# Batch 1 of a decay attention with its softmax weights turned by TensorE and float32 values

## The chip, the core and the metric

The kernel runs on one core of a Trainium2 chip. The core has five engines with a queue each, which run in order and wait for one another by semaphores: TensorE (PE, matmuls into PSUM), VectorE (DVE), ScalarE (ACT), GpSimd (POOL) and SyncE (SP, which here issues nearly all DMAs). The metric is the device time of one execution in microseconds; smaller is better.

## The reference

Attention with a decay for 8 batches of 8 heads, 576 tokens, 64 columns each, and then a feed-forward layer (FFN) over all 4608 tokens:

```python
scores = scale * np.matmul(q, k.transpose(0, 1, 3, 2))
log_f = np.log(np.clip(f, 0.0001, 1.0))
cum = np.cumsum(log_f, axis=-1)
decay = cum[:, :, :, None] - cum[:, :, None, :]
causal = np.triu(np.ones((S, S), dtype=bool), k=1)
scores = np.where(causal, -1000000000.0, scores + decay)
scores = scores - np.max(scores, axis=-1, keepdims=True)
attn = np.exp(scores)
attn = attn / (np.sum(attn, axis=-1, keepdims=True) + 1e-09)
...
x = np.ascontiguousarray(attn_out.transpose(0, 2, 1, 3)).reshape(B * S, H * D)
h = x @ w_in
g = np.maximum(h, 0.0) + np.log1p(np.exp(-np.abs(h)))
return (g @ w_out).astype(np.float32)
```

Here `w_in` is 512x2048 and `w_out` 2048x512. Everything is float32.

## The kernel before

**Attention.** Work is cut into jobs. Batch 0 has jobs of its own (`first`, `second`, `rest`, called plain): its scores are unsplit float32 products (L951), its softmax weights stay unnormalised, TensorE turns them with an identity matrix (`turn`, L1110), a copy brings them from PSUM to SBUF (`keep`, L1120, recorded as L254), and `output_tiled` multiplies them with float32 values (L1164) on two halves of the PE columns, 64 columns each. The division by the sums comes last (L1188).

From batch 1 on a job is one head (`whole`). q and k are split into a high and a low part by casts (L254) and subtractions (L907, L913), and the scores of a tile of query rows are two matmuls (L956, L957). `row_min` on DVE (L961) finds the row's extreme, ACT makes the exponentials and their sums (L989), `over` the reciprocals (L1002 to L1005). Then `turn_tile` normalises and splits each weight into two fp16 planes: the first part on ACT, POOL or DVE (L1037, L1039), the second on DVE (L1042). One DMA transpose per head (L1053, on SP's queue) turns both planes. The values are split in fp16 parts too (`split_v`, L874, L876, L880), with a scale by the largest value of each head, which `peak` finds with a DMA load and DVE reductions one batch ahead (L704 to L742). `output` multiplies (L1224, eleven matmuls), ACT scales one half of the result (L1244), DVE adds the other (L1248).

**FFN.** Tokens are taken in blocks: two of 128 in float32 (L1348, L1460), one of 256, then eight of 512. From the 256 block on each product is three matmuls of split operands: up (L1367, with the low weights from DRAM, `wl`), the activation on ACT and DVE (L1400 to L1420), down (L1441). A block can start when the attention of all its tokens is done. So block 256 to 511 needs batch 0, and the first block of 512 needs all heads of batch 1.

**Order.** Every operation is recorded in a plan with its predecessors, a cost and the buffers that it takes; `Plan.run` (L118) goes through the next 700 of them, always emits the one that can start earliest, and gives it to the engine that ends it first where there is a choice. What is emitted is a fixed order for each engine.

## Time and profile before

| | us |
|---|---|
| median of three runs | 1163.02 |
| lowest, highest | 1162.47, 1169.52 |
| the profiled execution | 1157.93 |
| its span, first to last instruction | 1156.1 |
| PE busy | 1094.2 |
| DVE busy | 882.3 |
| ACT busy | 808.6 |
| POOL busy | 231.6 |

The profile is one execution. Busy times count a matmul from its start to a modelled end, and neighbours overlap, so PE can be shown busy without running at its best. The clock column is what the throttle granted to TensorE, 1.00 being full speed. The rows that the prediction uses stand below, with the line numbers of the kernel before.

### The profile page before, as it was taken

To read this page: it belongs to the slowest core of one execution; us is meant where nothing else is said; L and a number is where in the kernel's file an instruction comes from. 1 tells how busy PE (TensorE), PEld (TensorE's weight loads), DVE (VectorE), ACT (ScalarE), POOL (GpSimd) and SP (SyncE) were. 2 spreads that over 40 slices of the span, in tenths; PEclk is the share of its full clock that TensorE was granted. 3 is DMA by queue.
4 is the path that set the end of the run, shared out by engine and by line. 5 is a ranking of instruction groups with operands and counts; after the bars stand their busy time and mean duration, and the time that the engine had idled before them with its cause. 6 is when DMAs were issued, how large, how long until landed. Compare 5 with 4: busy or idle time off the path is not lost. (4 is left out here: it accounts for less than half of the span.)

```text
span 1156.1 us, 17362 instructions
## 1 busy us (share of the span) xinstructions
PE 1094.2 (95%) x5452; PEld 849.8 (74%) x5452; DVE 882.3 (76%) x2169; ACT 808.6 (70%) x1867; POOL 231.6 (20%) x274
## 2 busy tenths in 40 slices
PE   8999787679998899999999999999999999999998
PEld 6776575557777677777777777777777777888886
DVE  7889899798888999989989888988898763223222
ACT  6888675657776677877778868877677775445444
POOL 3133222112221321212232121232233110000000
PEclk9999988888999899999999999999999999999999
DMA  9867688888977887869777977697669652112110
GB/s 246 247 201 225 199 207 212 203 204 188 213 177 168 183 214 185 200 156 227 182 168 172 228 177 176 151 221 172 154 143 219 152 121 90 43 55 73 55 55 37
DMA packets 278092, 193.55 MB, mean 167 GB/s; under 512 B 225216, under 2 KB 247008, under 8 KB 278000
## 3 DMA queue, kind: packets, MB, share of 16 engines
q1 hardware_dynamic: 277832, 192.29, 67.7%
q8 instruction: 43, 0.70, 0.2%
q14 instruction: 49, 0.40, 0.1%
q10 hardware_dynamic: 168, 0.15, 0.0%
HBM read 114.16 MB, written 14.83 MB: 112 GB/s over the span
## 5 line engine op out<-in xcount | busy, mean ns | idle before, releaser
L989 ACT ACTIVATE p<-s,negm 128x288 f32<-128x288 f32 (+7 forms) x384 | 184.2, 482 | 111.4 <-DVE negm L961 107.7
L1367 PE MATMUL h<-xh,wih 128*128 128x512 f32 (+1 forms) x576 | 228.0, 399 | 12.8 <-ACT p L989 4.8
L1367 PE MATMUL h<-xl,wih 128*128 128x512 f32 (+1 forms) x576 | 221.7, 388 | 2.3 <-DVE xl L1319 2.3
L1441 PE MATMUL acc<-woh_dt_float32r,gl 128*128 128x512 f32 x544 | 215.8, 397 | 7.4 <-DVE gl L1420 7.4
L1039 POOL TENSOR_SCALAR cross<-p,rsum 128x64 f16<-128x64 f32 (+4 forms) x146 | 139.8, 975 | 414.3 <-DVE rsum L1005 161.0
L1441 PE MATMUL acc<-woh_dt_float32r,gh 128*128 128x512 f32 x544 | 218.6, 402 | 2.3 <-ACT gh L254 1.4
L1441 PE MATMUL acc<-wol_dt_float32r,gh 128*128 128x512 f32 x544 | 215.0, 395 | 0.0
L1412 DVE SCALAR_TENSOR_TENSOR e<-h,e 128x512 f32<-128x512 f32 x136 | 93.2, 685 | 129.4 <-ACT e L1406 128.8
L1042 DVE SCALAR_TENSOR_TENSOR cross<-p,rsum,cross 64x64 f16<-64x64 f32 (+1 forms) x336 | 179.3, 569 | 14.4 <-POOL cross L1039 8.5
L961 DVE CUSTOM_DVE_ANT_0 s<-s,cmask 128x288 f32<-128x288 f32 (+6 forms) x320 | 135.6, 439 | 28.8 <-PE s L957 16.4
L1400 ACT ACTIVATE e<-h 128x512 f32<-128x512 f32 x144 | 85.6, 595 | 99.4 <-PE h L1367 96.3
L1367 PE MATMUL h<-xh,wl 128*128 128x512 f32 (+1 forms) x576 | 150.7, 384 | 1.1 <-DMA wl<-wil_d 1.1
L1367 PEld LDWEIGHTS h<-xh,wih 128*128 128x128 f32 x576 | 111.4, 193 | 34.8 <-ACT p L989 6.0
L1441 PEld LDWEIGHTS acc<-woh_dt_float32r,gl 128*128 128x128 f32 x544 | 103.7, 191 | 34.5 <-DVE gl L1420 12.1
L1367 PEld LDWEIGHTS h<-xl,wih 128*128 128x128 f32 x576 | 111.4, 193 | 22.2 <-DVE xl L1319 4.4
L254 ACT CAST gh<-e 128x512 fp32r<-128x512 f32 x128 | 79.2, 619 | 66.7 <-DVE e L1412 66.1
L1367 PEld LDWEIGHTS h<-xh,wl 128*128 128x128 f32 x576 | 106.5, 191 | 23.9 <-DMA wl<-wil_d 1.3
L1441 PEld LDWEIGHTS acc<-woh_dt_float32r,gh 128*128 128x128 f32 x544 | 103.9, 191 | 22.1 <-ACT gh L254 3.0
L956 PE MATMUL s<-T 128*64 128x64 f32 x336 | 105.8, 326 | 13.8 <-ACT e L1403 3.9
L1420 DVE TENSOR_TENSOR gl<-e,gh 128x512 fp32r<-128x512 f32 x136 | 93.8, 689 | 31.0 <-ACT gh L254 30.3
L1441 PEld LDWEIGHTS acc<-wol_dt_float32r,gh 128*128 128x128 f32 x544 | 103.9, 191 | 18.1
L957 PE MATMUL s<-T 68*64 68x64 f32 x336 | 100.5, 304 | 5.9 <-DVE T L913 5.6
(127 smaller groups left out, 1664.2 us busy)
## 6 DMA issues: line engine op xcount, KB each, us to landing
wl<-wil_d SPq DMA_DIRECT2D x72, 512.0 KB
raw<-in_qkT SPq DMA_DIRECT2D x112, 288.0 KB
vr<-in_vR SPq DMA_DIRECT2D x64, 160.0 KB
vp<-in_vR SPq DMA_DIRECT2D x28, 320.0 KB
out<-ob SPq DMA_DIRECT2D x35, 256.0 KB
T<-T SPq DMA_DIRECT2D x56, 144.0 KB
sto<-in_w_out SPq DMA_DIRECT2D x11, 512.0 KB
sti<-in_w_in SPq DMA_DIRECT2D x9, 512.0 KB
```

Source lines behind the costliest of these rows:

```text
L254: (e.tensor_copy if hasattr(e, "tensor_copy") else e.copy)(out, in_)
L956: e.matmul(o, qA[:, q0:end], kA[:, a:z], start=True, stop=False)
L957: e.matmul(o, qB[0:ST, q0:end], kB[0:ST, a:z], start=False, stop=True)
L961: e.tensor_tensor_reduce(out=box["o"], in0=box["o"], in1=cmask[0:n_q, right - w : right], scale=-0.125, scalar=m0 if i else 3.0e38, op0=AL ...
L989: e.activation(o, box["o"], AF.Exp, bias=m1, scale=-1.0, accum_out=acc)
L1039: e.tensor_scalar(to1, of, f_, None, ALU.mult)
L1042: e.scalar_tensor_tensor(to2, of, f_, to1, ALU.mult, ALU.subtract)
L1367: e.matmul(o, l, r, start=m == 0, stop=m == 11)
L1400: e.activation(box["e"], st["h", u], AF.Abs)
L1412: e.scalar_tensor_tensor(o, st["h", u], 0.0, box["e"], ALU.max, ALU.add)
L1420: e.tensor_sub(box["l"], box["e"], box["h"].bitcast(F32))
L1441: e.matmul(st["acc", tt], l, r[fc], start=first and m == 0, stop=last and m == 2,)
```

## The change

The eight heads of batch 1 become jobs `mixed`. Their scores, exponentials and sums stay as they were. Then the weights are normalised in place in float32 (`scale`: five instructions per head, on DVE, ACT or POOL), turned by TensorE in four banks per head (fifteen transposes), and copied to SBUF (four copies). The values are loaded into a float32 buffer and not split; `output_tiled` multiplies them in nine float32 matmuls on two column tiles, queries 0 to 383 on one and 384 to 575 on the other, and two copies (`take`) bring the result to its place. The fp16 planes, the DMA transpose, the split of the values and the search for their peaks are gone for batch 1, and stay for batches 2 to 7. The first bank has a tile of 68 rows of its own (`p64`), for the first 64 keys.

```diff
+    def mixed(h):
+        banks = [[(0, 0, 64, 0, 0), (512, 512, S, 0, 4)], [(0, 64, S, 0, 0)], [(128, 128, S, 0, 1)],
+                 [(256, 256, S, 0, 2), (384, 384, S, 0, 3)]]
+        return whole(1, h) | dict(
+            banks=banks, groups=[(0, 384, 0, 0), (384, S, 1, 0)],
+            puts=[(0, 384, h, 0), (64, S - 384, h, 384)],
+        )
...
+        mixed_ = not plain and b == 1
...
+                if mixed_:
+                    vtag = "vhl"
+                elif plain:
...
-            split_v()
+            if not mixed_:
+                split_v()
...
+            st["norm"] = []
+            for ti, (_, n_q, _, pi, po) in enumerate(tiles):
+                def scale(e, ti=ti, n_q=n_q, pi=pi, po=po):
+                    a, f_ = pt[pi][0:n_q, po : po + ends[ti]], rs[0:n_q, ti : ti + 1]
+                    if hasattr(e, "activation"):
+                        e.activation(a, a, AF.Copy, scale=f_)
+                    else:
+                        e.tensor_scalar(a, a, f_, None, ALU.mult)
+                st["norm"].append([add(scales(ends[ti]), scale, after=[r])])
...
+                        if small:
+                            x, one = pt[pi][:, c : c + ST], halves
+                            if key == 0:
+                                x, one = x[0:ST], ident[0:ST, 0:ST]
+                            blocks.append((x, key // 8, one))
...
-                    steps[bi].append(mm)
+                    steps[bi if plain else 0].append(mm)
...
-                            st["vr"][m["vc"][0]]["v"][:, m["vc"][1], :],
-                            m["p"]["p"][:, m["o"] : m["o"] + m["z"] - m["a"]],
+                            st["vr"][m["vc"][0]]["v"][0 : m["rows"], m["vc"][1], :],
+                            m["p"]["p"][0 : m["rows"], m["o"] : m["o"] + m["z"] - m["a"]],
...
+                def take(e, r=r, w=w, h=h, tok=tok):
...
+                    copy(e, to, box["ps"][r : r + 64, 0:w])
+                on = [on_act(w, psum=True), on_dve(w)]
+                d = add(on, take, after=before + x_taken.get(b, []), takes=takes)
...
-    jobs += [whole(b, h) for b in range(1, B) for h in range(H)]
+    jobs += [mixed(h) for h in range(H)]
+    jobs += [whole(b, h) for b in range(2, B) for h in range(H)]
...
-            if nstart <= n + H + 1 < len(jobs):
+            if nstart + H <= n + H + 1 < len(jobs):
```

How the order moves, at three places. The line numbers of the changed kernel are larger: its L965 to L971 are scores, L1145 turns, L1201 float32 values, L1421 and L1495 the FFN's up and down, L1036 is `scale`, L1003 the exponentials.

PE, third head of batch 1, before: the FFN's products (`acc`) and the scores (`s`) of the next head stand ahead of the fp16 values (`o_0`, `o_1`), which read the planes in `cross`.

```order
L1441 MATMUL acc_1_1788<-woh_dt_float32r,gl_2_1984 128x512
L956 MATMUL s_4_288_2057<-T_1297 128x288
L957 MATMUL s_4_288_2057<-T_1297 128x288
L1224 LDWEIGHTS v_17_1691
L1224 MATMUL o_0_2064<-cross,v_17_1691 128x64
```

The same engine in the changed kernel, between the heads of batch 1: the last values of one head (`o`), then the turning of the next (`b_0`, `b_1`), then a score of the one after.

```order
L1201 MATMUL o_1887<-cross,vr_1463 64x192
L1201 MATMUL o_1887<-cross,vr_1463 64x64
L1145 MATMUL b_0_1904<-ident,p_68_96 68x68
L1145 MATMUL b_0_1904<-halves,p_640_100 68x128
L1145 MATMUL b_1_1908<-ident,p_256_97 128x128
L1145 MATMUL b_1_1908<-ident,p_384_98 128x128
L1145 MATMUL b_1_1908<-ident,p_512_99 128x128
L1145 MATMUL b_1_1908<-ident,p_640_100 128x128
L970 MATMUL s_3_0_1917<-T_1080 128x448
```

The turning has come into PE's queue, ahead of scores that used to follow the values directly.

ACT at about the same head, before: first parts of the planes (`cross`) among exponentials, the result's scaling (`x`) and a cast of k or q.

```order
L989 ACTIVATE p_512_99,lsum_82<-s_3_0_2034,negm_78 128x448
L1037 ACTIVATE cross<-p_256_92,rsum_89 128x2x128
L1037 ACTIVATE cross<-p_384_93,rsum_89 128x3x128
L1244 ACTIVATE x_1_1646<-o_0_2064,v_down_113 64x64
L1037 ACTIVATE cross<-p_512_94,rsum_89 128x4x128
L254 CAST T_1078<-raw_2028 128x576
```

ACT in the changed kernel: normalising in place (`p`), and copies of turned banks (`cross<-b`).

```order
L1003 ACTIVATE p_640_100,lsum_80<-s_4_288_1788,negm_76 128x288
L254 CAST T_1307<-raw_1775 128x576
L1036 ACTIVATE p_68_96<-p_68_96,rsum_88 64x64
L254 COPY cross<-b_3_1840 128x512
L1036 ACTIVATE p_384_98<-p_384_98,rsum_88 128x320
L1036 ACTIVATE p_512_99<-p_512_99,rsum_88 128x448
L1036 ACTIVATE p_640_100<-p_640_100,rsum_88 128x576
L1003 ACTIVATE p_68_91,lsum_81<-s_0_0_1860,negm_77 64x64
```

Four of this head's five normalisations stand on ACT, where three first parts stood.

PE where the first block of 512 tokens begins (`h_0`), before: behind the values of batch 1's last head (`o_1`) and three scores of a head of batch 2.

```order
L1224 MATMUL o_1_2621<-cross,v_21_2218 128x64
L956 MATMUL s_0_0_2648<-T_1078 64x64
L957 MATMUL s_0_0_2648<-T_1078 64x64
L956 MATMUL s_1_0_2651<-T_1078 128x192
L957 MATMUL s_1_0_2651<-T_1078 128x192
L956 MATMUL s_2_0_2654<-T_1078 128x320
L957 MATMUL s_2_0_2654<-T_1078 128x320
L1367 MATMUL h_0_2663<-xh_2527,wih 128x512
```

The same place in the changed kernel: four scores of the same head of batch 2, and the last products of the block of 256 (`acc`).

```order
L970 MATMUL s_3_0_2688<-T_1080 128x448
L971 MATMUL s_3_0_2688<-T_1080 128x448
L1495 MATMUL acc_0_1874<-woh_dt_float32r,gh_7_2678 128x512
L1495 MATMUL acc_0_1874<-wol_dt_float32r,gh_7_2678 128x512
L1495 MATMUL acc_0_1874<-woh_dt_float32r,gl_7_2681 128x512
L1495 MATMUL acc_1_1875<-woh_dt_float32r,gh_7_2678 128x512
L1495 MATMUL acc_1_1875<-wol_dt_float32r,gh_7_2678 128x512
L1495 MATMUL acc_1_1875<-woh_dt_float32r,gl_7_2681 128x512
L1421 MATMUL h_0_2706<-xh_2629,wih 128x512
```

What has moved is the end of the block of 256, which is now the last thing ahead of the block of 512; the head of batch 2 has come about as far.

## Rows read from the trace of the kernel before

**Rows 1.** The page of the profile, busy tenths of PE and the granted TensorE clock in 40 slices of the span (one slice is 28.9 us).

```profile
PE   8999787679998899999999999999999999999998
...
PEclk9999988888999899999999999999999999999999
```

**Rows 2.** Busy time by stage (the view by windows): bounds in us, length, busy time of PE, PE's weight load, DVE, ACT and POOL with the number of instructions, the mean granted TensorE clock, the DMA engines' share, GB/s.

```profile
50.00:100.00 50.00, 49.29 (x318) 36.03 (x317) 45.24 (x103) 41.72 (x91) 14.71 (x18) 0.97 0.73 228
125.00:256.00 131.00, 101.86 (x534) 77.47 (x534) 116.36 (x312) 85.67 (x223) 30.69 (x33) 0.84 0.84 204
256.00:300.00 44.00, 38.73 (x179) 29.57 (x180) 37.67 (x88) 32.30 (x75) 10.12 (x10) 0.92 0.83 189
300.00:450.00 150.00, 142.51 (x686) 110.54 (x685) 132.51 (x329) 109.67 (x263) 37.66 (x42) 0.98 0.82 191
450.00:900.00 450.00, 440.98 (x2173) 344.51 (x2171) 394.09 (x995) 346.67 (x829) 110.88 (x112) 1.00 0.78 183
```

**Rows 3.** The same view for the stage 125 to 256 us, cut near the starts of its DMA transposes.

```profile
125.00:140.00 15.00, 13.11 (x60) 8.09 (x61) 13.98 (x44) 9.41 (x29) 4.96 (x6) 0.89 0.66 189
140.00:157.00 17.00, 11.35 (x53) 8.78 (x52) 16.42 (x43) 10.04 (x25) 2.38 (x3) 0.70 0.75 186
157.00:171.00 14.00, 13.63 (x92) 11.64 (x91) 12.24 (x33) 13.45 (x34) 5.18 (x5) 1.00 0.96 227
171.00:185.00 14.00, 7.97 (x40) 5.37 (x39) 13.57 (x36) 9.45 (x26) 4.79 (x3) 0.76 0.89 218
185.00:199.00 14.00, 10.87 (x62) 8.45 (x61) 12.94 (x33) 7.97 (x19) 3.17 (x4) 1.00 0.87 212
199.00:213.00 14.00, 9.18 (x52) 6.75 (x51) 10.39 (x31) 9.69 (x26) 3.64 (x4) 0.76 0.83 201
213.00:227.00 14.00, 12.29 (x81) 10.86 (x79) 9.35 (x30) 7.13 (x22) 1.98 (x2) 0.88 0.93 200
227.00:241.00 14.00, 10.67 (x47) 7.93 (x48) 13.13 (x32) 9.73 (x23) 2.85 (x3) 0.76 0.83 188
241.00:256.00 15.00, 12.79 (x63) 9.61 (x61) 14.34 (x39) 8.81 (x27) 1.74 (x3) 0.89 0.91 219
```

**Rows 4.** SyncE's queue in order of time: the DMA transposes of the first and of the last head of batch 1 (start us, us).

```profile
143.03 4.62 SPq L1053 DMA_TRANSPOSE cross<-cross  x1
...
241.36 5.31 SPq L1053 DMA_TRANSPOSE cross<-cross  x1
```

**Rows 5.** What PE waited for between 125 and 256 us (the view of waits: us in total, times, longest).

```profile
PE s L957 <- DVE T L913: 5.2, 5, 3.3
PE o L1224 <- DMA cross<-cross: 4.7, 2, 2.7
PE s L956 <- ACT e L1403: 3.9, 1, 3.9
```

**Rows 6.** DVE between 125 and 256 us, grouped by line: instructions, then busy us and mean ns of one, then idle time before them and what ended it.

```profile
L1042 DVE SCALAR_TENSOR_TENSOR cross<-p,rsum,cross 128x512 f16<-128x512 f32 (+4 forms) x54 | 27.0, 539 | 2.8 <-POOL cross L1039 1.8 <-ACT cross L1037 0.8
...
L1248 DVE SCALAR_TENSOR_TENSOR x<-o,v_down,x 64x64 f32<-64x64 f32 (+1 forms) x15 | 7.5, 498 | 0.9 <-ACT x L1244 0.6
...
L880 DVE SCALAR_TENSOR_TENSOR v<-vr,v_up,v 128x320 f16<-128x320 f32 x10 | 5.4, 542 | 0.0
```

**Rows 7.** ACT between 125 and 256 us, grouped by line and shape; same columns.

```profile
L1037 ACT ACTIVATE cross<-p,rsum 128x512 f16<-128x512 f32 x11 | 7.8, 717 | 0.1
...
L1244 ACT ACTIVATE x<-o,v_down 64x512 f32<-64x512 f32 x7 | 4.8, 684 | 1.4 <-PE o L1224 1.2
...
L1244 ACT ACTIVATE x<-o,v_down 64x64 f32<-64x64 f32 x8 | 2.5, 310 | 1.6 <-PE o L1224 1.5
...
L1037 ACT ACTIVATE cross<-p,rsum 64x64 f16<-64x64 f32 x3 | 1.0, 340 | 0.0
```

**Rows 8.** Copies of turned weights out of PSUM (batch 0) and casts of q and k, whole span, grouped by line and shape; same columns.

```profile
L254 ACT CAST T<-raw 128x576 fp32r<-128x576 f32 x60 | 39.2, 667 | 7.2 <-PE s L956 3.6 <-DMA raw<-in_qkT 2.7 <-DMA vr<-in_vR 0.8
...
L254 ACT COPY cross<-b 128x512 f32<-128x512 f32 x9 | 5.2, 578 | 2.8 <-PE b L1113 2.8
L254 DVE COPY cross<-b 128x512 f32<-128x512 f32 x7 | 4.7, 675 | 0.0
```

**Rows 9.** PE in order of time where a head of batch 0 is turned, and where its values are multiplied (start us, us, what, number).

```profile
105.24 0.28 PE L1110 MATMUL b<-ident,p 128*128 128x128 f32 x1
...
105.46 0.93 PE L1110 MATMUL b<-ident,p 128*128 128x128 f32 x7
106.23 1.02 PE L1460 MATMUL acc<-wol_dt_float,g 128*128 128x512 f32 x2
...
112.60 1.31 PE L1164 MATMUL o<-cross,vr 128*64 128x192 f32 x18
```

**Rows 10.** The granted clock while PE ran those (the view by windows).

```profile
105.00:109.00 4.00, 3.49 (x23) 2.56 (x22) 3.97 (x12) 4.00 (x11) 2.05 (x4) 1.00 0.93 291
```

**Rows 11.** PE in order of time at the values of the first head of batch 1.

```profile
153.97 0.33 PE L1224 MATMUL o<-cross,v 128*128 128x64 f16 x2
...
156.00 1.45 PE L1224 MATMUL o<-cross,v 128*128 128x512 f16 x9
```

**Rows 12.** PE in order of time where the first block of 512 tokens begins.

```profile
260.13 0.50 PE L1367 MATMUL h<-xh,wih 128*128 128x512 f32 x1 [2.67 <-ACT xh L254]
261.78 0.80 PE L1367 MATMUL h<-xl,wih 128*128 128x512 f32 x1 [1.15 <-DVE xl L1319]
```

More of the change, by code (lines that the diff above doesn't have):

```diff
@@ L298, in tile_decay_attention_softplus_ffn @@
                 x32=2, wl=2, vhl=3, vraw=1, vpk=1, raw=1)
-    plan = Plan(BUFS | dict(bank=6, acc=2, acc2=0, T0=4, stat=4, p=2, xh0=1, xh1=1, xl0=1, ph=3, pl=3, one=2, pp=1, pT=1))
+    plan = Plan(BUFS | dict(bank=6, acc=2, acc2=0, T0=4, stat=4, p=2, xh0=1, xh1=1, xl0=1, ph=3, pl=3, one=2, p64=2, pp=1, pT=1))
     add, give = plan.add, plan.give
@@ L350, in tile_decay_attention_softplus_ffn @@
     rsum = [cpool.tile([P, 5], F32, name=f"rsum{i}") for i in range(4)]
-    PW = [64] + [128 * (i + 1) for i in range(1, 5)]
+    PW = [ST] + [128 * (i + 1) for i in range(1, 5)]
     ps = [[cpool.tile([P, w], F32, name=f"p{i}_{w}") for w in PW] for i in range(2)]
@@ L387, in tile_decay_attention_softplus_ffn @@
         one=[cross[:, 3200 + P * i : 3200 + P * i + P] for i in range(2)],
+        p64=[cross[:, i : i + P] for i in (3456, 3712)],
     )
@@ L1002, in over @@
                 e.scalar_tensor_tensor(a, a, 1e-9, z, ALU.add, ALU.add)
-                if not plain:
+                if not plain and not mixed_:
                     e.tensor_scalar(a, a, 1.0 / UP, None, ALU.mult)
@@ L1013, in finish_stats @@
             st["over"] = r
+            if not mixed_:
+                return
+            st["norm"] = []
[7 more added lines that the diff above has]
+                st["norm"].append([add(scales(ends[ti]), scale, after=[r])])
+            give("stat", [x for xs in st["norm"] for x in xs])
         def turn_tile(ti):
@@ L1069, in weights @@
                 w += hi - lo
+            small = mixed_ and bi == 0
             blocks, need = [], []
             for ti, (q0, n_q, k0, pi, po) in enumerate(tiles):
-                for key, lo, hi, _, at in reversed(spans):
+                for key, lo, hi, _, at in spans if small else reversed(spans):
                     if q0 < hi and q0 + n_q > lo and k0 <= key:
@@ L1081, in weights @@
                         c = po + key - k0
-                        one = halves if second else ident
-                        blocks.append((pt[pi][:, c : c + P], at, one))
+                        if small:
[3 more added lines that the diff above has]
+                            blocks.append((x, key // 8, one))
+                        else:
+                            one = halves if second else ident
+                            blocks.append((pt[pi][:, c : c + P], at, one))
                         need += st["norm"][ti]
             box = {}
-            sums = job["sums"].get(bi, [])
+            sums = job["sums"].get(bi, []) if plain else []
             if sums:
@@ L1113, in turn @@
                     e.transpose(box["ps"][:, at1 + at : at1 + at + m], one, ident[0:m, 0:m])
-            tag = tags[bi] = ("ph", "pl")[count["p"] % 2]
-            count["p"] += 1
+            tag = tags[bi] = "p64" if small else ("ph", "pl")[count["p"] % 2]
+            count["p"] += not small
+            rows = ST if small else P
             def keep(e):
                 box["p"] = slice_of(tag, used[bi])[:, 0:w]
-                copy(e, box["p"], box["ps"][:, 0:w])
+                copy(e, box["p"][0:rows], box["ps"][0:rows, 0:w])
             need = list(dict.fromkeys(need)) + halves_set
@@ L1129, in weights @@
                 give("p", st["turned"])
-                give("stat", st["turned"])
+                if plain:
+                    give("stat", st["turned"])
             on = [on_act(w, psum=True), on_dve(w)]
@@ L1134, in weights @@
             for key, lo, hi, vc, at in spans:
-                parts.append((lo, hi, bi, vc, at, box, ready))
+                parts.append((lo, hi, bi, vc, at, box, ready, rows))
         def output_tiled():
@@ L1142, in output_tiled @@
                 todo.sort(key=lambda x: (max(x[0], g0) > g0, x[2]))
-                for lo, hi, bi, vc, at, pbox, ready in todo:
+                for lo, hi, bi, vc, at, pbox, ready, rows in todo:
                     a, z = max(lo, g0), min(hi, g1)
@@ L1180, in output_tiled @@
             puts = []
-            for r, rows, c, w, bi, o, h, tok in job["puts"]:
+            for r, w, h, tok in [] if plain else job["puts"]:
+                def take(e, r=r, w=w, h=h, tok=tok):
+                    if b not in x_of:
+                        x_of[b] = buf("x32", [P, NCC, S], f"x32_{b}")
+                    to = x_of[b][64 * (h % 2) : 64 * (h % 2) + 64, h // 2, tok : tok + w]
+                    copy(e, to, box["ps"][r : r + 64, 0:w])
+                takes = () if b in x_taken else ("x32",)
+                on = [on_act(w, psum=True), on_dve(w)]
+                d = add(on, take, after=before + x_taken.get(b, []), takes=takes)
+                x_taken.setdefault(b, [d])
+                puts.append(d)
+                wrote.setdefault(b, []).append((tok, tok + w, d))
+            for r, rows, c, w, bi, o, h, tok in job["puts"] if plain else []:
                 def put(e, r=r, rows=rows, c=c, w=w, bi=bi, o=o, h=h, tok=tok):
@@ L1198, in output_tiled @@
             give("att", puts, back(box, "ps"))
-            if quad:
+            if mixed_:
+                give("T", st["scores"])
+                give("vhl", before)
+            elif quad:
                 s_of[heads[0]] = s_of[heads[2]] = st["scores"], before
@@ L1276, in attention @@
             s=[lambda ti=ti: stat_tile(ti) for ti in range(nt)],
-            w=[lambda bi=bi: weights(bi) for bi in range(len(banks))] if plain
+            w=[lambda bi=bi: weights(bi) for bi in range(len(banks))] if plain or mixed_
             else [lambda ti=ti: turn_tile(ti) for ti in range(nt)],
-            o=[output_tiled] if plain else [lambda gi=gi: output(gi) for gi in range(len(groups))],
+            o=[output_tiled] if plain or mixed_ else [lambda gi=gi: output(gi) for gi in range(len(groups))],
         )
```

3 lines of the change are left out of this document (1 added, 2 removed).

## The prediction

> **What bounds the kernel now.** I read the page's slices first, then busy times by stage, then what PE waits for. The slices show PE at nine or ten tenths from about 290 us to the end, and at six to nine tenths with a reduced clock between about 125 and 290 us [rows 1]. By stage this is plainer. From 300 to 900 us PE is busy 142.51 of 150 us and 440.98 of 450 us at a clock of 0.98 and 1.00, so there the kernel is as long as PE's work. From 125 to 256 us PE is busy 101.86 of 131 us at a mean clock of 0.84, while DVE is busy 116.36, which is 89% [rows 2]. That stage is the attention of batch 1: its eight DMA transposes are issued between 143.03 and 241.36 us [rows 4], one head in 14 us ((241.36 - 143.03) / 7). The only FFN work that may run beside it is the block of 256 tokens and what is left of the two float32 blocks. The first block of 512 waits for batch 1 and starts at 260.13 us [rows 12].
>
> What PE waits for in the stage is mostly DVE and the transposes: 5.2 us for the low part of k (L913), 4.7 us for `cross` from the DMA, 3.9 us once for a stretch that an exponential of the FFN ended [rows 5]. Each pause has a second price. In the pieces with pauses (140 to 157, 171 to 185, 199 to 213, 227 to 241) the granted clock was 0.70 to 0.76, a mixture of its two levels, 1.2 and 2.4 GHz; in the dense piece from 157 to 171 it was 1.00 [rows 3]. Busy time times clock, summed over the nine pieces, gives 87.5 us of PE work at full clock in 131 us, a share of 67%. So some 43 us of PE are lost in this stage, and DVE sets its pace.
>
> **The change, part by part.** Counting the two programs' orders, the changes are of batch 1 alone.
>
> DVE loses 48 second parts of planes at 0.539 us, 16 additions of results at 0.498 and 8 low parts of values at 0.542 [rows 6]: 25.9 + 8.0 + 4.3 = 38.2 us. It gains 22 copies from PSUM, at most 0.675 each [rows 8], so 14.9. Net it falls by 23 us or a little more (some small operations, and the peaks of batch 1, go too): from 116 to 93.
>
> ACT loses 25 first parts and gains 30 normalisations. Both lie between 0.340 us for 64 columns and 0.717 for 512 [rows 7]; at their middle, 0.53, that is +2.6. It loses 8 scalings at 0.684 and 8 at 0.310 [rows 7], 8.0 together, and gains 26 copies at up to 0.578 and 6 casts at 0.667 [rows 8], 15.0 + 4.0. Net +13.6: from 85.7 [rows 2] to 99. The ten normalisations that the order puts on POOL replace 22 first parts there and are hidden, since POOL is busy 30.69 of 131 us [rows 2].
>
> PE gains 15 transposes per head, 120 in all. Seven in a row end 0.93 us after the first starts, and the next matmul begins 0.77 us after it [rows 9], 0.11 us each: 13.2 us. The upper bound is the duration of a single one, 0.28 us [rows 9], if nothing overlapped: 33.6 us. I take 0.11, because the turning in the changed order comes in groups of two to six, nearly as in that row. The values hardly change. Before, they take 0.33 + 1.45 = 1.78 us per head [rows 11]. After, nine float32 products on two column tiles: in batch 0 the longer tile of such nine has 640 columns and takes 1.31 us [rows 9]; here it has 832, so 1.31 x 832 / 640 = 1.70. I count nothing for the 0.08. PE's work in the stage becomes 87.5 + 13.2 = 100.7 us.
>
> DMA: the transposes leave SP's queue, where each held it for 4.6 to 5.3 us ahead of the next loads [rows 4]. The stage moved 204 GB/s with them and an earlier one 228 [rows 2], so the loads alone fit in a shorter stage.
>
> The sum. The work that must fit is now PE 100.7, ACT 99, DVE 93, against PE 87.5, ACT 86, DVE 116. The longest is PE, so the question is how densely it packs. In the stage from 300 to 450 us its share is 142.51 x 0.98 / 150 = 93%, from 50 to 100 us 96%, from 450 to 900 us 98% [rows 2], each with DVE at 88 to 90%. But in none of these is ACT above 83% (41.72 of 50), and here it would be 90%. So I take a little less than the lowest of them, 91%: 100.7 / 0.91 = 110.7 us in place of 131, which is 20.3 us earlier.
>
> From there on nothing gives it back. At the start of the block of 512 the two orders have about the same head of batch 2 in hand, and the values of each later head stand behind the same number of FFN products as before, to within 18 of them (4 us) up to batch 4 and exactly from there on (counted in the two orders). PE is the bound there with the same work, so all of it moves up by 20.3 us. The profiled execution would take 1157.9 - 20.3 = 1137.6. The median of the three runs is 5.1 us above that execution (1163.0 against 1157.9), so the forecast is 1142.7 us.
>
> **A rule against the change.** Seven transposes take 0.77 us to the next matmul, while the granted clock was 1.00 [rows 9, 10]. The Trainium skill, TensorE: Matmul & The Clock Gate, section Part 4: PE-mode transpose, gives about 275 ns for a 128x128 transpose in a kernel and says that the full clock does not engage for transposes. By that figure the turning would be an estimated 33 us, about the upper bound above, and the gain would be gone. The trace disagrees in both points for groups inside other matmuls. No row shows long turning alone.
>
> **Rivals.**
>
> *ACT or the chain becomes the bound (0.21).* A head now goes from reciprocal to five normalisations, turning, copies and values, four of the five on ACT between exponentials, and PE's queue is in order, so scores behind a turn wait with it. For it: ACT rises by 14 us to the highest share of any stage, and 3.9 us of today's waits already end on ACT [rows 5]. Against it: a transpose of 4.6 us or more and its wait disappear from the same chain. PE's share would be 79 to 86%, the stage 127.5 to 117.1 us, the time 1149 to 1159.5.
>
> *More than the stage (0.12).* PE packs at 98% as later (102.8 us, gain 28.2), and the loss at the start of the block of 512 shrinks, where 44 us hold 38.73 x 0.92 = 35.6 of work [rows 2] and PE waits 2.67 us for the cast on ACT [rows 12]. Gain 28 to 36.6, time 1126 to 1135. Against it: the cast stays where it is.
>
> *The turning does not overlap (0.06).* At 0.28 us each, PE's work is 87.5 + 33.6 = 121.1, the stage 121.1 / 0.91 = 133.1, the time 1165.
>
> *Slower: PE still stands in pauses at the low clock (0.06).* If PE's share stays at 67%, because each turn waits on scales and then on copies as the values waited on the DMA, the added 13.2 us of work are paid at that share: 100.7 / 0.668 = 150.7 us, 19.7 more, time 1183. It decides from the point where PE's share is below 100.7 / 131 = 77%. Against it: the pauses are DVE's and the transposes', and both get less.
>
> **How the numbers follow.** The forecast case (0.55) is a PE share of 86 to 98%, 1135 to 1149 us, with 1142.7 inside. The range takes in the two neighbours, the ACT rival whole and most of the larger gain: 1129 to 1160, leaving out the last two rivals and the far end of the third, some 0.17. A measurement of this kernel tells about 1% from no change, 11.6 us. Faster than 1151.4 are the forecast, the larger gain and about a quarter of the ACT rival: 0.55 + 0.12 + 0.06 = 0.73. Within 1% are the rest of it and the unoverlapped turning: 0.15 + 0.06 = 0.21. Slower by more than 1%: 0.06.
>
> **What would show it.** Right: the first 512-wide product starts near 240 us in place of 260; between 125 us and that point PE's clock is near 1.00 and its share above 85%, DVE is busy some 93 us and ACT some 99; groups of transposes advance by 0.11 us each. After it, stages look as before, 20 us earlier. Wrong: PE waits named after `scale` or after copies of banks, a clock still at 0.75 in pieces, or batch 2's heads late so that the block of 512 runs out of neighbours.

## The result, and the profile after

| | before | after |
|---|---|---|
| median, us | 1162.7 (1153.2 to 1169.5, 4 runs) | 1121.2 (1119.3 to 1122.0, 4 runs) |
| profiled execution, us | 1157.9 | 1119.3 |
| mean granted clock | 0.973 | 0.997 |

The ratio of the times is 0.965, 95% interval 0.958 to 0.972: 41 us faster between the medians, 38.6 us between the profiled executions. The forecast was 20.3. The kernel before was measured again beside every experiment; its medians there, of 7 to 25 runs, were 1155.8 to 1159.2 us, so a few of the 41 us are the spread of four runs, and 3 us between kernels of different sets are not told from none.

The slices of the changed kernel's page, of PE and its clock, answer [rows 1]:

```profile
PE   8999999999999999999999999999999999999998
PEclk9899999999999999999999999999999999999999
```

The valley from 125 to 290 us is gone. By windows (columns as in [rows 2]), with the stage of batch 1 now ending at 227.7 us:

```profile
50.00:100.00 50.00, 49.07 (x341) 36.07 (x341) 45.46 (x111) 43.48 (x98) 14.14 (x18) 1.00 0.71 213
125.00:227.70 102.70, 100.05 (x707) 83.69 (x707) 93.70 (x248) 86.56 (x234) 21.36 (x21) 1.00 0.70 196
227.70:271.70 44.00, 43.20 (x213) 33.66 (x212) 40.01 (x100) 35.42 (x83) 8.95 (x10) 1.00 0.88 201
271.70:421.70 150.00, 145.16 (x719) 111.91 (x718) 135.27 (x335) 114.28 (x274) 36.31 (x40) 1.00 0.81 189
421.70:871.70 450.00, 437.58 (x2154) 341.56 (x2153) 388.78 (x976) 346.64 (x830) 109.14 (x111) 1.00 0.77 181
```

The second row is the one to read. PE is busy 100.05 of 102.70 us, 97.4%, at the full clock; DVE is busy 93.70 and ACT 86.56. In the whole stage PE waits 2.5 us (against the list in [rows 5]; engine, line, releaser, us in total, times, longest):

```profile
PE h L1421 <- DVE e L1466: 1.1, 1, 1.1
PE s L970 <- ACT p L1003: 0.7, 2, 0.4
PE h L1421 <- ACT cross L254: 0.4, 1, 0.4
PE h L1421 <- ACT p L1003: 0.3, 1, 0.3
```

The first 512-wide product (timeline of PE; start, duration) comes directly behind FFN products and waits for nothing, where [rows 12] shows 2.67 and 1.15 us of waiting:

```profile
227.90 0.40 PE L1495 MATMUL acc<-woh_dt_float32r,gl 128*128 128x512 f32 x1
228.14 0.39 PE L1421 MATMUL h<-xh,wih 128*128 128x512 f32 x1
228.37 0.39 PE L1421 MATMUL h<-xl,wih 128*128 128x512 f32 x1
```

That is 32.0 us earlier than 260.13. Of the two waits of [rows 12] only the first, 2.67 us, lies in these 32.0; the second, 1.15, came behind that product. The last values of all, before and after, start 38.7 us earlier, so another 6.7 us were won behind the start of the wide block:

```profile
958.05 1.45 PE L1224 MATMUL o<-cross,v 128*128 128x512 f16 x9
```

```profile
919.33 1.45 PE L1278 MATMUL o<-cross,v 128*128 128x512 f16 x9
```

One head's turning and values (same view, for [rows 9] and [rows 11]):

```profile
147.31 0.38 PE L1145 MATMUL b<-halves,p 128*128 128x128 f32 x2
147.53 0.49 PE L1145 MATMUL b<-ident,p 128*128 128x128 f32 x3
147.78 0.36 PE L1421 MATMUL h<-xh,wih 128*128 128x256 f32 x1
...
149.88 1.64 PE L1201 MATMUL o<-cross,vr 68*64 68x64 f32 x18
151.45 0.36 PE L970 MATMUL s<-T 128*128 128x192 f32 x1
```

Five transposes advance PE by 0.47 us, 0.09 each; all 120 of the stage, in 18 groups of 2 to 15, advance it by 12.6 us, 0.105 each. The nine value products on two column tiles, 18 records, take 1.64 (1.70 had been worked out).

### The profile page after: what moved, and what is told of

Same layout as the page of the kernel before. It is cut to its first block, busy times and chain, and to the rows that moved or that the text cites. A ratio compares the mean times of both kernels' runs of the same rounds, so it can differ in the third digit from the quotient of the medians.

```text
span 1117.5 us, 17615 instructions
## 1 busy us (share of the span) xinstructions
PE 1086.7 (97%) x5628; PEld 851.8 (76%) x5628; DVE 849.8 (76%) x2094; ACT 810.5 (73%) x1886; POOL 216.8 (19%) x256
## 4 chain that ended last, share of the span: by engine, by line
PE 46%; DVE 31%; DMA 7%; ACT 7%; issue 5%; POOL 2%; SPq 1%; DVEq 0%; POOLq 0%; ACTq 0%
PE h L1421 18%; PE acc L1495 15%; DVE cross L1070 5%; DVE s L975 5%; DMA cross<-cross 4%; DVE e L1466 3%; PE o L1278 2%; PE h L1402 2%; ACT p L1003 2%; DVE gl L1474 2%; DVE T L920 2%; DVE T L926 2%; DMA vp<-in_vR 2%; DVE x L1302 2%; PE acc L1514 2%
## 5 line engine op out<-in xcount | busy, mean ns | idle before, releaser
L1003 ACT ACTIVATE p<-s,negm 128x288 f32<-128x288 f32 (+7 forms) x384 | 183.6, 481 | 82.8 <-DVE negm L975 75.7
L1421 PE MATMUL h<-xh,wih 128*128 128x512 f32 (+1 forms) x576 | 225.1, 394 | 9.6 <-DVE e L1466 4.6
L1421 PE MATMUL h<-xl,wih 128*128 128x512 f32 (+1 forms) x576 | 218.6, 382 | 0.5 <-DVE xl L1373 0.4
L1495 PE MATMUL acc<-woh_dt_float32r,gh 128*128 128x512 f32 x544 | 216.1, 397 | 0.2 <-ACT gh L254 0.2
L1495 PE MATMUL acc<-woh_dt_float32r,gl 128*128 128x512 f32 x544 | 213.1, 392 | 3.0 <-DVE gl L1474 3.0
L1495 PE MATMUL acc<-wol_dt_float32r,gh 128*128 128x512 f32 x544 | 212.7, 391 | 0.0
L1067 POOL TENSOR_SCALAR cross<-p,rsum 128x512 f16<-128x512 f32 (+4 forms) x124 | 118.4, 970 | 330.4 <-DVE rsum L1019 164.5
L1070 DVE SCALAR_TENSOR_TENSOR cross<-p,rsum,cross 128x512 f16<-128x512 f32 (+4 forms) x288 | 154.9, 572 | 13.8 <-POOL cross L1067 10.6
L1421 PE MATMUL h<-xh,wl 128*128 128x512 f32 (+1 forms) x576 | 149.0, 380 | 0.0
L1421 PEld LDWEIGHTS h<-xh,wih 128*128 128x128 f32 x576 | 108.6, 188 | 31.5 <-DVE e L1466 4.6
L1421 PEld LDWEIGHTS h<-xl,wih 128*128 128x128 f32 x576 | 108.6, 188 | 20.2 <-DVE xl L1373 2.4
L1495 PEld LDWEIGHTS acc<-woh_dt_float32r,gl 128*128 128x128 f32 x544 | 102.1, 188 | 27.8 <-DVE gl L1474 5.7
L1421 PEld LDWEIGHTS h<-xh,wl 128*128 128x128 f32 x576 | 104.9, 188 | 22.5
L1495 PEld LDWEIGHTS acc<-woh_dt_float32r,gh 128*128 128x128 f32 x544 | 102.4, 188 | 19.7 <-ACT gh L254 1.1
L1495 PEld LDWEIGHTS acc<-wol_dt_float32r,gh 128*128 128x128 f32 x544 | 102.4, 188 | 17.9
L970 PE MATMUL s<-T 128*64 128x64 f32 x336 | 102.7, 317 | 7.1 <-DVE e L1466 3.6
L971 PE MATMUL s<-T 68*64 68x64 f32 x336 | 97.4, 295 | 0.0
```

The lines of the kernel that those rows point to most:

```text
L970: e.matmul(o, qA[:, q0:end], kA[:, a:z], start=True, stop=False)
L971: e.matmul(o, qB[0:ST, q0:end], kB[0:ST, a:z], start=False, stop=True)
L1003: e.activation(o, box["o"], AF.Exp, bias=m1, scale=-1.0, accum_out=acc)
L1067: e.tensor_scalar(to1, of, f_, None, ALU.mult)
L1070: e.scalar_tensor_tensor(to2, of, f_, to1, ALU.mult, ALU.subtract)
L1421: e.matmul(o, l, r, start=m == 0, stop=m == 11)
```

## Experiments I: parts put back into the changed kernel

Each expectation states the theories that it separates; A is that DVE's work set the pace of the stage. What is "lost" or "gained" here is counted from the changed kernel's 1121.2 us. Of each change the main lines are shown; ... stands for lines left out.

**e1.** The DVE work of the second parts, on a tile that nobody reads:

```
+ def second(e, ti=ti, n_q=n_q, pi=pi, x=x, n=n):
+     of, j = pt[pi][0:n_q, x : x + n], junk[0:n_q, 0:n]
+     e.scalar_tensor_tensor(j, of, rs[0:n_q, ti : ti + 1], j, ALU.mult, ALU.subtract)
...
+ on = On("DVE", 0.12 + n / 960, 0.0, True)
+ extra.append(add(on, second, after=st["norm"][ti] + junk_set))
...
+ give("p", st["turned"] + st.get("extra", []))
```

> The changed kernel, with six more DVE instructions per head of batch 1 of the shapes of the second parts that the change removed; they write a scratch tile that nobody reads. Theory A (the stage is as long as its busiest engine, and the change helps because it takes work off DVE): DVE's 93.7 us in the stage go up by 48 x 0.539 x 0.88 = 22.8 to 116, above PE's 100, so the stage grows by 15 to 28 us and pauses and a lower clock come back: 1136 to 1149 us. Theory B (the pauses came from the DMA transposes, which held SP's queue and the values): DVE has room, 1121 to 1126 us.

1142.1 us (1139.9 to 1143.9), 21 us of the 41 lost, as theory A had it. The last line also lets go of the weights' buffer only behind the added work, as the second parts did before. Its window from 125 to 256 us has DVE at the old 116 us again and PE at a clock of 0.93:

```profile
125.00:256.00 131.00, 112.96 (x720) 92.69 (x719) 116.32 (x293) 89.83 (x236) 27.35 (x28) 0.93 0.55 148
```

**e4.** The search for the peaks of batch 1's values kept, its result unused:

```
- if nstart + H <= n + H + 1 < len(jobs):
+ if nstart <= n + H + 1 < len(jobs):
```

> The changed kernel, with the search for the largest values of batch 1 kept though nobody uses it (four loads of 320 KB, a store, a spread, and about 6 us of DVE at 100 to 126 us). If this search, ahead of the stage, is what made the gain larger than the stage's part (theory C): 1125 to 1128 us. If it was hidden: 1120 to 1123 us.

1131.8 us, above both ranges, but its four runs stand apart, 1124.5 and 1127.2 against two of 1136.3, so about 10 us lost is a loose figure. Where this search can hurt is seen on DVE in the kernel before, at the end of batch 0:

```profile
122.29 2.03 DVE L733 TENSOR_REDUCE v_down<-vs 128x8 f32<-128x1024 bf16 x1 [1.32 <-DMA vs<-v_d]
...
126.06 0.69 DVE L1412 SCALAR_TENSOR_TENSOR g<-h,e 128x512 f32<-128x512 f32 x1
```

From 120.97 to 126.06 DVE waits for the exchanged peaks and works on scales, but for one instruction on the FFN's weights, and the product of the gate behind them (L1412) is what PE waits 2.4 us for. The changed kernel does not wait there; its last values of batch 0 start at 127.58 us in place of 134.34. In e4's own trace the same reduction stands at 131.55 us and PE waits for the gate again:

```profile
135.85 1.10 PE L1514 MATMUL acc<-wol_dt_float,g 128*128 128x512 f32 x2 [1.58 <-DVE g L1466]
```

Its first wide product starts at 238.72 us, 10.6 late, with both waits back (2.12 and 1.69 us). The wait of 1.58 us is a small part of that; the rest is a new order, and which part of it costs was not tried.

**e5 and e6.** The turning of batch 1 done twice (120 more transposes), and the value products of one column tile after those of the other:

```
- for x, at, one in blocks:
+ for x, at, one in blocks * (2 if mixed_ else 1):
...
- step = [m for ms in zip_longest(*sides) for m in ms if m]
+ step = sides[0] + sides[1] if mixed_ else [m for ms in zip_longest(*sides) for m in ms if m]
```

> The changed kernel, with every transpose of batch 1 done twice into the same place: 120 more transposes on PE and nothing else. If PE sets the pace of the new stage and transposes advance by 0.11 us: 13.2 us more, 1133 to 1136 us. If the stage still has room on PE: 1121 to 1126 us. If transposes cost 0.28 us each: 1150 us and more.

> The changed kernel, with the nine value products of a head of batch 1 issued for one column tile after the other, not in turns. If the two tiles run side by side only when they alternate, a head's values go from 1.64 us to about 1600 columns x 4 / 2400 = 2.67 us, 8 us in all: 1128 to 1131 us. If the order does not matter: 1120 to 1123 us.

e5: 1130.5 us (1126.8 to 1132.9), 9.3 lost, between its two ranges: most of the 13.2 us is paid, not all. From 125 to 256 us PE has no room left:

```profile
125.00:256.00 131.00, 127.84 (x905) 110.01 (x902) 108.89 (x283) 106.24 (x278) 30.53 (x28) 1.00 0.67 182
```

e6: 1130.6 (1124.7 to 1135.8), 9.4 lost, as expected; its nine products take longer than the 1.64 above:

```profile
160.15 2.34 PE L1201 MATMUL o<-cross,vr 68*64 68x64 f32 x18
```

Eight times 0.70 is 5.6 us of PE. Both say that in the stage PE's work is now paid for, as the prediction had it: PE is the bound there.

**e7.** Batch 2 done in the new way too:

```
- mixed_ = not plain and b == 1
+ mixed_ = not plain and b <= 2
```

> The changed kernel, with batch 2 made like batch 1 too. Theory A, PE being 97 to 98% busy at full clock from 228 us on: the 120 transposes are paid in full, 13 us, 1133 to 1136 us. Rival: less work on DVE and on the DMAs pays again, 1105 to 1120 us.

1124.2 us (1123.9 to 1130.9), in neither range, and 3 us above the change, which is no more than sets differ. Batch 2 has the wide block beside it and PE was nearly full there already; its 13.2 us of added turning cost less than their sum, so some was given back, but no gain shows.

## Experiments II: parts left out of the kernel before

**e2, e3, e8**, each one removal alone, the order of all queues planned anew by the kernel's planner:

```
+ if b == 1 and heads[0]:                     # e2: no second parts
+     st["split"].append(a)
+     continue
...
+ if b == 1 and heads[0]:                     # e3: no DMA transpose
+     st["cross"] = [add(NO_ENGINE, mark, after=st["split"], takes=("pT",), lag=0.0)]
...
+ e.memset(v_up[1], 2.0**13)                  # e8: constant scales, no peaks of batch 1
+ e.memset(v_down[1], 2.0**-28)
```

> The kernel before, without the second parts of the planes for seven of batch 1's eight heads (their low planes are stale, so their weights are rounded). 42 DVE instructions go, some 20 us of DVE's 116 in the stage; the DMA transposes stay and PE gets no new work. Theory A: the stage shrinks from 131 to about 100 to 108 us, 1132 to 1140 us in all. Theory B: the values still wait for the transposes, 1154 to 1163 us.

> The kernel before, without the DMA transposes of seven of batch 1's eight heads (their values read the first head's turned planes); DVE's work is unchanged. Theory A: DVE still has 116 us in the stage, 1157 to 1163 us. Theory B: SP's queue is free and nothing waits for a transpose, 1130 to 1145 us.

> The kernel before, with a constant in place of the largest values of batch 1 as the scale of its fp16 values; the four loads, the spread and about 6 us of DVE go. Theory C: the batch begins 3.6 to 6.8 us earlier, 1154 to 1159 us. If it was hidden: 1160 to 1163 us.

e2: 1164.5 us, ratio 1.006 (1.003 to 1.010), nothing gained. e3: 1150.5, ratio 0.993 (0.989 to 0.996), in neither range. e8: 1157.3, ratio 1.000 (0.998 to 1.003), nothing gained beside its own runs of before. In e2 the transposes show that batch 1 did run faster (the eighth issued at 222.09 us in place of 241.36), but the wide block came only 11 us earlier and batches 2 and 3 gave all of it back by some 490 us. Theory A, by which e2 had to gain over 20 us, fell. e3 shows the same from the other side. It keeps all of DVE's work, and in its new order the first wide product starts at 248.15 us, 12.0 earlier, with DVE fuller than it was before (the stage up to 4.1 us ahead of that product, as in [rows 2]):

```profile
125.00:244.00 119.00, 97.52 (x533) 76.03 (x533) 114.12 (x301) 86.91 (x224) 40.55 (x38) 0.87 0.61 167
```

DVE is busy 96% of it; so the 89% of before was not DVE's limit.

**e9, e10, e11, e15.** To see whether the new planning had spoilt e2, the order of every engine was held, and the instructions in heads 1 to 7 were made short in place: second parts of one column per block (e9), transposes of one block of 30 (e10), both (e11), both and the additions of results (e15):

```
+ if b == 1 and heads[0]:
+     to2, of, to1 = to2[..., 0:1], of[..., 0:1], to1[..., 0:1]     # e9, e11, e15
...
+     to, x = to[:, 0:1], planes[:, 0:P]                            # e10, e11, e15
...
+ z = 1 if b == 1 and heads[0] else w                               # e15: columns of the addition
```

> The kernel before with the order of every engine kept as it is; the 42 second parts of planes of heads 1 to 7 of batch 1 write one column of each block in place of all (so these weights are rounded to fp16). DVE loses about 42 x 0.45 = 19 us of the stage from 125 to 256 us and the fill of a head's planes gets a little shorter. Theory A (DVE's work alone set the pace, and run e2 missed because the planner had put other work in another order): the first wide product 18 to 22 us earlier, 1136 to 1145 us. Theory L (two bounds stand close together in this stage: DVE's work of 116 us, and a loop of the one buffer of planes, which is filled in some 6 us and held some 7 us until its transpose has landed, 13 to 14 us per head, 8 heads; either alone keeps the stage long): the heads come every 11.5 us or so as in e2, at most 10 us gained, 1148 to 1160 us.

> The kernel before with the order of every engine kept; the DMA transposes of heads 1 to 7 of batch 1 move one block of 30 (the values read the planes of the first head). DVE keeps its 116 us. Theory A: no gain beyond 3 us, 1156 to 1163 us. Theory L: the loop of the planes falls by some 4 us per head, DVE's work is what is left, 116 us at a share near 95 percent, so some 8 to 12 us gained, 1147 to 1153 us, as in e3.

> The kernel before with the order kept, and both left out in heads 1 to 7 of batch 1: second parts of one column, transposes of one block. Theory A: as e9 (1136 to 1145), no more. Theory L: both bounds are gone, PE's work of 87.5 us at a share of 93 percent or more is what is left of 131 us, the clock in the stage above 0.95, the first wide product near 225 to 232 us, 1118 to 1132 us: a gain of about that of the whole change, from work that is left out and not replaced. If the two only add (9 us each or less), 1141 to 1150 us.

> The old order kept (as e11), second parts of one column, transposes of one block, and additions of results of one column. Theory O: 1148 to 1158 us, hardly less than e11, though DVE is relieved of 27 us. Theory R: 1140 us or less.

1156.2, 1156.7, 1154.8 and 1153.8 us, ratios 0.997, 0.998, 0.996 and 0.998: nothing to speak of. Theory L, by which e11 had to come below 1132 us, fell with A. A short second part still takes DVE some time: the 54 of the stage take 13.8 us in e11 (L1044), 27.0 before. The window of e11 from 125 to 256 us:

```profile
125.00:256.00 131.00, 102.53 (x540) 78.31 (x538) 106.99 (x314) 85.98 (x222) 28.68 (x32) 0.85 0.59 157
```

No engine is above 82%, and still the heads come every 13.6 us (transposes from 140.78 to 236.03 us, seven steps), 14.0 before. What holds them is read from DVE's timeline in e11, one head:

```profile
183.14 0.76 DVE L907 TENSOR_TENSOR T<-raw,T 64x576 fp32r<-64x576 f32 x1
183.93 0.75 DVE L913 TENSOR_TENSOR T<-raw,T 64x576 fp32r<-64x576 f32 x1
...
186.85 1.47 DVE L636 TENSOR_TENSOR wol_dt_float32r<-wol,woh_dt_float32r 128x512 fp32r<-128x512 f32 x1
188.25 0.21 DVE L961 CUSTOM_DVE_ANT_0 s<-s,cmask 64x64 f32<-64x64 f32 x1
...
194.35 0.76 DVE L1254 SCALAR_TENSOR_TENSOR x<-o,v_down,x 64x512 f32<-64x512 f32 x1 [0.86 <-ACT x L1250]
...
195.40 0.54 DVE L880 SCALAR_TENSOR_TENSOR v<-vr,v_up,v 128x320 f16<-128x320 f32 x1
195.97 0.76 DVE L907 TENSOR_TENSOR T<-raw,T 64x576 fp32r<-64x576 f32 x1
```

and from ACT and PE beside it:

```profile
188.55 0.31 ACT L989 ACTIVATE p<-s,negm 64x64 f32<-64x64 f32 x1 [3.89 <-DVE negm L961]
```

```profile
184.73 0.24 PE L957 MATMUL s<-T 68*64 68x64 f32 x1 [0.48 <-DVE T L913]
```

Low parts of q and k at 183.14, the scores that PE waits to begin, row maxima from 188.25 (ACT waits 3.89 us for them), then an older head's results and values, and only behind these the next head's low parts at 195.97: 12.8 us around, on a queue that runs in order. Between scores and row maxima DVE works 2.6 us on the FFN's weights (185.70 to 188.32), though the first scores end at 184.97. In this head DVE is itself busy 11.06 of the 12.83 us: the loop is a chain of its instructions, in the order planned for the old work, with waits in between. That this chain holds every head is read from one head, not shown by e11.

**e12, e13, e14.** The same removals with a new order, and two more: second parts and transposes (e12), results in one plane as well (e13), constant scales as well (e14). The edits are those of e2 and e3, then

```
+ d = c                                    # e13: no addition of the second plane
+ if b != 1 or not heads[0]:
+     d = add(On("DVE", 0.136 + w / 960), put, after=[c])
```

and that of e8.

> The kernel before without the second parts and without the DMA transposes of heads 1 to 7 of batch 1 (the values read the planes of the first head), the order of all queues planned anew for this. Runs e9 to e11 kept the old order and gained 0 to 4 us, so neither DVE's work nor the transposes set the pace in that order. Theory O (the in-order queues do: each head's low parts of q and k stand on DVE's queue behind the row maxima of the head before and the results of an earlier one, and the loop through scores, maxima and back takes a head's 13 us; only a new order shortens it, and the planner makes one when the work is gone): the first wide product near 225 to 238 us, 1125 to 1142 us. Theory R (the results and values in two planes hold the loop): 1147 us or more, as in e2 and e3.

> As e12, and the 14 additions of the second plane of results are left out too (results of heads 1 to 7 are one plane). Planned anew. Theory O: 2 to 6 us below e12. Theory R: 1120 to 1135 us, 12 us or more below e12.

> As e13, and the peak search of batch 1's values replaced by a constant scale. What is left of the change's removals is the split of the values. Planned anew. PE has 87.5 us of work left in the stage, 13 less than in the changed kernel, so if nothing else holds it, 1105 to 1120 us under both theories; if it stays above 1140 us, what the change adds (copies, turning on PE) matters and not only what it removes.

| heads 1 to 7 of batch 1 without | old order | new order |
|---|---|---|
| second parts | 1156.2 (e9) | 1164.5 (e2) |
| transposes | 1156.7 (e10) | 1150.5 (e3) |
| both | 1154.8 (e11) | 1142.0 (e12) |
| and second results | 1153.8 (e15) | 1135.9 (e13) |
| and peaks | | 1126.3 (e14) |

The ratios of e12 to e14 are 0.985 (0.981 to 0.988), 0.981 (0.977 to 0.984) and 0.972 (0.967 to 0.977). Nearly the same work left out (short instructions stay in the old order) is worth 4 us in the old order and 17 in a new one (e11, e12; each against its own runs of before), 5 and 23 with the second results (e15, e13). All removals together, with nothing put in their place, bring 33. e12 and e13 end within 1 us of theory O's ranges (that the order of the queues holds the heads), and R, by which e13 had to come 12 us below e12, is not borne out. e14 is in neither of its ranges: with 13 us less work for PE than the changed kernel it is 5 us slower. In these new orders DVE is again the fullest engine up to the wide block (e14):

```profile
125.00:233.00 108.00, 94.18 (x539) 71.12 (x540) 99.67 (x267) 81.48 (x215) 34.36 (x37) 0.94 0.72 195
```

That is 92% of DVE, and 93 and 94% in e12 (106.02 of 113.50 us) and e13 (99.47 of 106.00).

## Experiments III: the order alone, and one place of it

**e16.** All the work of before, but the planner counts it in batch 1 as if second parts and additions cost 0.06 us and a transpose landed at once.

```
+ add(On("DVE", 0.06 if b == 1 else 0.12 + w / 960, 0.0, True), second_part, after=[a])
...
+ st["cross"] = [add(on_cross(), send, after=st["split"], takes=("pT",), lag=0.0 if b == 1 else CROSS)]
...
+ d = add(On("DVE", 0.06 if b == 1 else 0.136 + w / 960), put, after=[c])
```

> The kernel before with all its work, but the planner is told that in batch 1 the second parts and the additions of results cost 0.06 us of DVE and that a transpose lands at once, so it writes an order as for a batch without them. If the old order is itself what holds the heads (order alone): 10 us or more faster, below 1150 us. If order and work must change together (less work in the old order gained 0 to 5 us, e9 to e11 and e15; less work in a new order 17 to 33, e12 to e14): no gain, 1155 to 1175 us, since DVE still has its 116 us and the transposes still take their time.

1176.8 us, ratio 1.015 (1.010 to 1.020). The first wide product starts at 276.52 us. A new order without less work is worse: the old one was right for the old work.

**e17.** How the orders differ is plainest on DVE where the next head's low parts stand. Rows of its order before (a head's first and last row maxima, then the low parts, then the next head):

```
333 L961 ISA s_0_0_1561,negm_75<-s_0_0_1561,cmask 64x64
...
345 L961 ISA s_4_288_1598,negm_75<-s_4_288_1598,cmask,negm_75 128x288
...
354 L907 TENSOR_TENSOR T_1297<-raw_1593,T_1297 64x576
...
365 L961 ISA s_0_0_1715,negm_76<-s_0_0_1715,cmask 64x64
```

and in the changed kernel:

```
341 L975 ISA s_0_0_1723,negm_76<-s_0_0_1723,cmask 64x64
...
343 L920 TENSOR_TENSOR T_1080<-raw_1628,T_1080 64x576
...
361 L975 ISA s_4_288_1788,negm_76<-s_4_288_1788,cmask,negm_76 128x288
...
369 L975 ISA s_0_0_1860,negm_77<-s_0_0_1860,cmask 64x64
```

Before, they stand behind the last maxima; now, in this head, right behind the first. The experiment puts this place back into the changed kernel:

```
+ behind = last_max if mixed_ and heads[0] else []     # the row maxima of the head before
+ q2 = add(lo_on, q_lo, after=[q1, *behind])
...
+ k2 = add(lo_on, k_lo, after=[k1, *behind])
...
+ last_max[:] = st["min"]
...
- units += [prep] + s_ + o_
+ late_prep = nstart <= n < nstart + H - 1
+ units += s_ + [prep] + o_ if late_prep else [prep] + s_ + o_
```

> The changed kernel with all its work and one thing put back as it stands in the order before: in heads 1 to 7 of batch 1 the low parts of q and k of the next head (lines 920 and 926) may start on DVE only behind the last row maxima of the head before; in the changed kernel's order they stand right behind its first. Loop theory (this place closes a loop of low parts, scores, exponentials, maxima and low parts again, 12 to 13 us a head in run e11, so that two heads can hardly overlap): waits of PE for low parts come back, the granted clock in the stage falls below 0.97, 1127 to 1145 us. If the place of the low parts does not matter and only the amount of work does: 1119 to 1125 us.

1135.3 us (1130.8 to 1137.7), 14 lost with no work added. The last two lines also record the whole preparation of a head, casts included, behind the scores of the head before, so a little more than one place moves. The time is that of the loop theory; the way is only partly. PE's waits are not named after low parts (the largest, 2.9 us in four, are turns that wait for an exponential), and the clock falls at the end of the stage rather than in all of it (windows):

```profile
125.00:200.00 75.00, 72.48 (x509) 59.11 (x509) 65.93 (x169) 57.52 (x153) 13.39 (x10) 1.00 0.67 192
200.00:235.00 35.00, 31.46 (x204) 26.20 (x204) 27.89 (x77) 26.59 (x74) 7.22 (x8) 0.95 0.56 147
235.00:256.00 21.00, 18.32 (x74) 13.95 (x75) 17.21 (x40) 13.87 (x32) 3.47 (x4) 0.84 0.81 168
```

The wide block begins 7.9 us later, and its two waits are back:

```profile
236.07 0.77 PE L1423 MATMUL h<-xh,wih 128*128 128x512 f32 x1 [2.23 <-DVE lsum L1018]
238.45 0.79 PE L1423 MATMUL h<-xl,wih 128*128 128x512 f32 x1 [1.61 <-DVE xl L1375]
```

## Why the prediction was right or wrong

**The direction and the mechanism of the end were right.** PE becomes the bound of the stage. Its work was worked out as 100.7 us at full clock and is 100.05; DVE's as 93 and is 93.70; the transposes as 13.2 us and advance PE by 12.6; the values as 1.70 and are 1.64. DVE's number is in part luck: 19 copies take 9.9 us where 22 had been priced at 14.9, the work left out was 35.0 in the stage and not 38.2, and the reductions of the peaks rise there from 6.0 to 8.6 us. The rivals that turning does not overlap, and that PE stays in pauses at the low clock, are refuted by the same rows; so is the one by which ACT becomes the bound (0.21), with ACT busy 86.56 of 102.70 us and 1.4 us of PE's waits that end on ACT. That the trace disagrees in both points with the Trainium skill was said too strongly: the duration of a single transpose agrees (last section). The larger gain (28 to 36.6 us, chance 0.12) named two of its three sources, a share of 98% and the wide start; the measured one lies past its far end.

**The step that failed is PE's share of 91%.** It is 97.4%: 100.05 / 0.974 is 102.7 us where the sum had 110.7. That is 8.0 us. The share was put low because ACT was expected at 99 us, 90% of the stage. It is 86.56, next to nothing above before, and 84% of the stage. ACT's groups in the stage show why (line, operation, count, busy, mean ns):

```profile
L1036 ACT ACTIVATE p<-p,rsum 128x576 f32<-128x576 f32 (+4 forms) x30 | 14.7, 553 | 1.4 <-DVE v_down L747 1.1 <-DVE rsum L1019 0.2
...
L254 ACT COPY cross<-b 128x512 f32<-128x512 f32 (+2 forms) x22 | 10.2, 483 | 0.4 <-PE b L1145 0.2
...
L254 ACT COPY x<-o 64x384 f32<-64x384 f32 (+1 forms) x8 | 3.1, 393 | 1.6 <-DVE x L254 1.2 <-PE o L1201 0.2
```

Those three add 28.0 us. In the same view of before, from 125 to 256 us, stand 30 first parts, 15 scalings of results and 7 first planes of values, 27.4 us together:

```profile
L1037 ACT ACTIVATE cross<-p,rsum 128x512 f16<-128x512 f32 (+3 forms) x30 | 16.2, 588 | 0.1
...
L1244 ACT ACTIVATE x<-o,v_down 64x64 f32<-64x64 f32 (+1 forms) x15 | 7.3, 484 | 3.0 <-PE o L1224 2.7
...
L874 ACT ACTIVATE v<-vr,v_up 128x320 f16<-128x320 f32 x7 | 3.9, 562 | 5.9 <-DVE v_up L741 2.4 <-PE o L1224 2.3 <-DMA T<-aug_d 1.1
```

The sum had counted 25 first parts, had forgotten the planes of values, had priced the copies at 0.578 where they took 0.48 and 0.39, and had added six casts that the stage does not show (11 casts of q and k in either kernel). That PE packs less densely beside a fuller ACT was itself assumed, and no run tried it.

**Two terms were missing.** "From there on nothing gives it back" holds, but behind the stage more is won: 3.7 us at the wide start, 2.67 of them the wait that is gone, and 6.7 us behind it, with the second wait of 1.15 us among them. Before lost time there as well: from 350 to 375 and from 375 to 400 us PE was busy 22.11 and 21.73 of 25 us, the second at a clock of 0.86; the changed kernel has 24.17 and 24.36 at 1.00. With these the account closes: 20.3 + 8.0 + 3.7 + 6.7 = 38.7. No PE work was done ahead for it: PE's busy time by clock up to 125 us is about the same, 45.73 x 0.93 + 49.07 + 25.00 = 116.6 us after and 46.45 + 49.29 x 0.97 + 23.72 = 118.0 before (windows 0 to 50, 50 to 100 and 100 to 125 us). The clock dips once in either profile, from 58 to 66 us before (0.80) and from 30 to 50 us after (0.75, then 0.91). The dip before comes and goes in kernels that hold its order, 1.00 in e11 and 0.88 in e9, so 1 to 3 us of a single profile may be chance.

**The picture of before was wrong.** "DVE sets its pace" was read from a busy share of 89%. e9, e11 and e15 bring DVE's busy time from 125 to 256 us from 116.36 to 107.74, 106.99 and 104.91 in the old order and gain 3 to 5 us, and in e3 the same DVE work fits a stage 12 us shorter. So DVE's work did not set the pace by itself: the order of the queues, planned for that work, held the heads too. The loop through DVE's queue is how that looks in one head of e11; it is argued, and e17 supports one link of it. The forecast came out with the right sign because the planner wrote a new order for the new work, which the prediction took for granted: the sign was in part luck. DVE's work still counts in a new order: e1 loses 21 us by it, and in e12 to e14 DVE is 92 to 94% busy. e14 shows that the removals in a new order bring most of the gain (33 us, with the split of the values still there), e16 that the order alone does not.

**Open.** e17 shows that the place of the low parts is worth 14 us in the changed kernel, not that it is the whole difference between the orders. Of the 19 us that e2's eighth transpose was early, 8 were gone at the wide block and 11 in batches 2 and 3; why was not tried. Nor is it shown how the 6.7 us behind the wide start were won.

## What to carry to other kernels

An engine at 89% in a stage need not be its bound: make its instructions short in place, with the order held, and see whether the stage gets shorter. Where queues run in order, look for the loop from one head's (or tile's) first instruction to the next one's on the same queue; here work taken out gained at most 5 us while the order stayed and up to 33 in a new one, and a new order for less work lost time while the work was still there. Price an added instruction on a full engine by all rows that the same view shows to leave, counted in that view and not from the code.

## What the runs showed of the hardware that was not expected

Turning on PE in groups among other matmuls ran at a granted clock of 1.00 through a whole stage, 120 transposes and, in e5, 240 (clock 1.00 from 125 to 256 us). The Trainium skill, TensorE: Matmul & The Clock Gate, section Part 4: PE-mode transpose, has some 275 ns for a 128x128 transpose in a kernel and no full clock. The first agrees with the duration of a single one here, 0.27 us, but in groups they advanced PE by 0.105 us each, which is what a sum has to count. The second is not what this stage shows; its longest group was 15 transposes in 1.9 us, and no run shows long turning alone.

Two column tiles of 64 whose products alternate took 1.64 us for the nine of a head; the same products one tile after the other took 2.34. Busy times of rows on ACT overlap: the groups of the stage before add up to 99.6 us, and the engine was busy 85.67; 11.7 of the 99.6 are reads of an accumulated sum, 0.2 us each.
